# A fused attention and token/channel mixer kernel: load order, the first pairs' engine assignment, and the homes of one addition and three casts

## The chip, the cores and the metric

The kernel runs on one core of a Trainium2 chip. Its time is the device time of one execution in microseconds. Five engines work side by side, each with a queue of its own that runs in order: PE (matrix multiply), DVE (vector), ACT (scalar functions), POOL (GpSimd), and SP, which here only issues DMAs. An engine waits at the head of its queue until what it needs is done; everything behind it waits too.

## The reference

Cosine attention over 8 batches and 12 heads, 448 positions, head size 64, followed by a mixer over tokens and channels:

```python
q_n = q / (norm(q) + 1e-06); k_n = k / (norm(k) + 1e-06)
attn = softmax(q_n @ k_n.T / tau)
x = (attn @ v) rearranged to [batch, 448, 768]
u = x + (relu(x.T @ w_tok1) @ w_tok2).T
out = u + relu(u @ w_ch1) @ w_ch2
```

w_tok1 is 448 x 256 and w_tok2 256 x 448 (the small weights); w_ch1 is 768 x 1536 and w_ch2 1536 x 768. All are float32 in memory; the kernel multiplies in float16.

## The kernel before, in words

**Pairs.** The 96 heads are worked off as 48 pairs (N = 48, six per batch, NPAIR = 6), in a software pipeline whose iteration i does the scores of pair i, the attention output of pair i - 1, and prepares pairs i + 1 to i + 3. The order of all instructions is written out by hand: `tc.manual_schedule()` keeps each engine's queue in program order, and waits are added where data or a buffer is needed.

For one pair the steps are: `load` (q, k, v, 224 KB each, from SP, L164), `squares` (L175 on ACT or L177 on POOL), `norm_sum` (DVE, L187, 16 sums of 64 squares), `norm_root` (ACT, a logarithm and an exponential, L191 and L192), `norm_rec` (DVE, L197 adds 1e-6 and L199 is the reciprocal), `normalize` (q and k times their reciprocal norms into float16, L211), a transpose of both (PE into PSUM, L238, then a copy to `qkT`, by DVE at L246 or ACT at L244), `score` (four matmuls for each half, L257, into two PSUM buffers `pS`), `expo` (ACT, L264, four per pair), `v_cast` (v to float16, by ACT at L220 or by DVE through `recast`, a tensor_reduce over one element, L128), and `pv` (32 matmuls, L278, then DVE's reciprocal at L284 and multiplication into `x` at L285).

**Iterations.** Iterations 0 to 12 are `opening(i)`; from 13 on it is `slot(i)`, where the channel mixer's matmuls of earlier batches (`ch1` L375, `ch2` L384) fill PE between the attention's steps. Batch 0's token mixer is done pair by pair in the opening: `tok1_pair` (L347, L349), `tok2_pair` (L358, into the PSUM tile `pU`) and `u_pair` (L366), which adds `x` to `pU` twice: once into float16 `u16`, which SP then transposes into `uT` (L368), and once into float32 `u32`. In iteration 6 (NPAIR) pairs 4 and 5 are both finished, so four such additions stand in a row. The first `ch1` matmuls follow in iteration 8.

**Before iteration 0** the program lists the loads, and then the norms, the normalization and the transposes of pair 0 and the norms of pair 1. `normalize(0, True)` gives q to POOL in one instruction, and half of k to each of POOL and DVE. The weights go through float32 staging tiles: `w1_load` (eight DMAs, the last 64 rows twice because batches with an odd number use them in the other half of the partitions), `w2_load` (one DMA of 448 KB). They are cast by `w1_cast` (DVE, two instructions at the end of iteration 1) and `w2_cast` (ACT, iterations 1 and 2). w_ch1 and w_ch2 are loaded by POOL's queue (`wide`) in iterations 1 to 11.

The DMAs that SP issues share eight completion counters in turn, so a DMA is issued only after the one eight places earlier has landed. Tiles come from rotating pools: five buffers each for q, k and v, two for `sq`, two for `pS`, four PSUM buffers under the tag `ps` for `pT`, `pO`, `pR`, `pU`, `pG` and `pF`.

Of the kernel before, what the change touches and what calls it, by code (L numbers as in the profile page):

```python
# [9 lines left out]
FP32 = mybir.dt.float32  # L10
FP16 = mybir.dt.float16
AF = mybir.ActivationFunctionType
ALU = mybir.AluOpType
# [5 lines left out]
def _bcast_free(ap: bass.AP, n: int) -> bass.AP:  # L19
    return bass.AP(tensor=ap.tensor, offset=ap.offset, ap=list(ap.ap) + [[0, n]])  # L20
# [3 lines left out]
def kernel(  # L24
# [19 lines left out]
    nc = tc.nc  # L44

    B, H, S, E = q.shape
    D = H * E
    T = moe_w_tok1.shape[1]
    C = moe_w_ch1.shape[1]
    P = 112  # L50
    NCH = S // P
# [3 lines left out]
    NPAIR = H // 2  # L55
# [7 lines left out]
    att = ctx.enter_context(tc.tile_pool(name="att", bufs=3))  # L63
    mix = ctx.enter_context(tc.tile_pool(name="mix", bufs=1))
# [6 lines left out]
        name=nc.get_next_instruction_name(), act_func_set_id=ACT_SET_LN_EXP,  # L71
# [15 lines left out]
    w1t = cst.tile([128, 5, T], FP16, name="w1t")  # L87
# [4 lines left out]
    stage = {}  # L92
# [5 lines left out]
    def ident():  # L98
        nc.gpsimd.memset(id16[:], 0.0)
        nc.gpsimd.affine_select(out=id16[:], in_=id16[:], compare_op=ALU.not_equal,  # L100
                                fill=1.0, base=0, pattern=[[-1, 128]], channel_multiplier=1)
        for t in v16s:
            nc.gpsimd.memset(t[:, :, E:E + 1], 1.0)
        st = mix.tile([128, 5, T], FP32, name="w1s", tag="u32", bufs=2)
        stage["w1"] = st
        nc.gpsimd.memset(st[64:128, 3, :], 0.0)
        nc.gpsimd.memset(st[0:64, 4, :], 0.0)

    def w1_load(n):
        st = stage["w1"]  # L110
        rows = moe_w_tok1.rearrange("(p c) t -> c p t", c=NCH)
        if n < 3:
            for f, m in f_segments(128 * n, 128 * n + 128):
                c, p = f // P, f % P
                nc.sync.dma_start(out=st[f - 128 * n:f - 128 * n + m, n, :],
                                  in_=rows[c, p:p + m, :])
        else:
            nc.sync.dma_start(out=st[0:64, 3, :], in_=rows[3, P - 64:P, :])
            nc.sync.dma_start(out=st[64:128, 4, :], in_=rows[3, P - 64:P, :])

    def w2_load():
        st = mix.tile([128, TT, S], FP32, name="w2s", tag="u32", bufs=2)
# [3 lines left out]
    def recast(out, in_):  # L126

        nc.vector.tensor_reduce(out=out, in_=bass.AP(tensor=in_.tensor, offset=in_.offset,  # L128
                                                     ap=list(in_.ap) + [[1, 1]]),
                                axis=AXX.X, op=ALU.max)  # L130

    def w1_cast(z):
        a, o = (t[:].rearrange("p n t -> p (n t)") for t in (stage["w1"], w1t))
        h = 5 * T // 2
        recast(o[:, z * h:(z + 1) * h], a[:, z * h:(z + 1) * h])

    def w2_cast(tt):
        nc.scalar.copy(out=w2t[:, tt, :].rearrange("k (c p) -> k c p", c=NCH),
# [21 lines left out]
    def load(i, names="qkv"):  # L160
        b, pj = pairs[i]
        for nm in names:
            t = ld.tile([P, 2, NCH, E], FP32, name=f"{nm}l", tag=f"{nm}l")
            nc.sync.dma_start(  # L164
                out=t[:].rearrange("p g c e -> p g (c e)"),
                in_=src[nm][b, 2 * pj:2 * pj + 2].rearrange("g (p c) e -> p g (c e)", c=NCH))
            st_[i][nm] = t

    def squares(i, act=""):
        s = st_[i]  # L170
        s["sq"] = att.tile([P, 2, 2 * NCH, E], FP32, name="sq", tag="sq", bufs=2)
        for j, nm in enumerate("qk"):
            a = s[nm][:].rearrange("p g c e -> p (g c) e")
            if nm in act:
                nc.scalar.activation(out=s["sq"][:, j], in_=a, func=AF.Square)  # L175
            else:
                nc.gpsimd.tensor_mul(out=s["sq"][:, j], in0=a, in1=a)  # L177

    def small(i, nm):
        if nm not in st_[i]:  # L180
            st_[i][nm] = att.tile([P, 2, 2 * NCH], FP32, name=nm, tag=nm)
        return st_[i][nm]

    BOTH = slice(0, 2)

    def norm_sum(i, j=BOTH):
        nc.vector.tensor_reduce(out=small(i, "ssq")[:, j], in_=st_[i]["sq"][:, j], axis=AXX.X,  # L187
                                op=ALU.add)

    def norm_root(i, j=BOTH):  # L190
        nc.scalar.activation(out=small(i, "ln")[:, j], in_=small(i, "ssq")[:, j], func=AF.Ln)  # L191
        nc.scalar.activation(out=nns[i % 3][:, j, :, 0], in_=small(i, "ln")[:, j], func=AF.Exp,  # L192
                             scale=0.5)

    def norm_rec(i, j=BOTH):

        nc.vector.tensor_reduce(out=small(i, "nre")[:, j], in_=nns[i % 3][:, j], axis=AXX.X,  # L197
                                op=ALU.add)
        nc.vector.reciprocal(out=small(i, "rn")[:, j], in_=small(i, "nre")[:, j])  # L199

    def normalize(i, vec):
        s = st_[i]
        t = att.tile([P, 2, NCH, 2, E], FP16, name="qkn", tag="qkn")
        for j, nm in enumerate("qk"):
            for g in ((0, 1) if vec and j else (BOTH,)):
                eng = nc.vector if g == 1 else nc.gpsimd
                rn = small(i, "rn")[:, j].rearrange("p (g c) -> p g c", g=2)[:, g]
                o = t[:, j, :, g, :]
                if g == BOTH:
                    o = o.rearrange("p c g e -> p g c e")  # L210
                eng.tensor_tensor(out=o, in0=s[nm][:, g], in1=_bcast_free(rn, E), op=ALU.mult)  # L211
        s["qkn"] = t

    def v_cast(i, act):
        s = st_[i]
        s["v16"] = v16s[i % 4]
        a = s["v"][:].rearrange("p g c e -> p (g c) e")
        o = s["v16"][:, :, 0:E]
        if act:
            nc.scalar.copy(out=o, in_=a)  # L220
        else:
            recast(o, a)
# [5 lines left out]
            out=s["T"][:].rearrange("d j (c p) -> d (j c) p", c=NCH),  # L228
            in_=s["qkn"][:].rearrange("p j c g e -> p (j c g e)"))

    def tpose_pe(i, act=False):
        s = st_[i]
        s["T"] = att.tile([128, 2, S], FP16, name="qkT", tag="qkT")
        for js in ((slice(0, 1), slice(1, 2)) if act else (BOTH,)):
            pt = ps.tile([128, 2, NCH, P], FP16, name="pT", tag="ps")
            for j in range(js.start, js.stop):
                for c in range(NCH):
                    nc.tensor.transpose(pt[:, j, c, :],  # L238
                                        s["qkn"][:, j, c].rearrange("p g e -> p (g e)"),
                                        id16[:P, :P])  # L240
            o, a = s["T"][:, js].rearrange("d j s -> d (j s)"), \
                pt[:, js].rearrange("d j c p -> d (j c p)")
            if act:
                nc.scalar.copy(out=o, in_=a)  # L244
            else:
                nc.vector.tensor_copy(out=o, in_=a)  # L246

    def score(i, g):

# [177 lines left out]
    todo, held, first = [], [], []  # L427
# [12 lines left out]
    eps()  # L440
    load(1, "qk")
    ident()
    load(0, "v")
    load(2, "qk")
    load(1, "v")
    load(3, "qk")
    for n in range(4):
        w1_load(n)
    w2_load()
    load(4, "qk")  # L450
    for n in (2, 3, 4):
        load(n, "v")
    squares(0, act="qk")
    for j in range(2):
        norm_sum(0, j)
        norm_root(0, j)
    for j in range(2):
        norm_rec(0, j)
    squares(1, act="qk")
    normalize(0, True)  # L460
    tpose_pe(0, act=True)
    norm_sum(1)
    norm_root(1)
    norm_rec(1)
    squares(2)
# [4 lines left out]
    def opening(i):  # L470

        normalize(i + 1, False)
        score(i, 0)
        norm_sum(i + 2)
        expo(i, 0)
        expo(i, 1)
        if not i:
            v_cast(0, True)
        norm_root(i + 2)
        v_cast(i + 1, i in (0, 2, 3, 4, 5))  # L480
        squares(i + 3)
        if i in wide:
            wide[i]()
        fill()
        if i >= 1:
            pv(i - 1, 0)
            pv(i - 1, 1)
        norm_rec(i + 2)
        if i in (1, 2):
            w2_cast(i - 1)  # L490
        r_, u_, add = first[0] if first else (None,) * 3
        done = [i - 2] if 2 <= i <= NPAIR else []
        if done:
            r_(i - 2)
        fill()
        score(i, 1)
        expo(i, 2)
        expo(i, 3)
        tpose_pe(i + 1)
        if i == NPAIR:  # L500
            r_(i - 1)
            done.append(i - 1)
        for pj in done:
            u_(pj)
        for half in (True, False):
            for pj in done:
                add(pj, half)
        if i == 1:
            w1_cast(0)
            w1_cast(1)  # L510
        fill()
        fill()
        fill()
# [98 lines left out]
```

## Time and profile before

| what | us |
|---|---|
| three timed runs | 409.12, 411.62, 411.42; median 411.42 |
| the profiled execution | 409.57 |
| its span in the profile | 407.2 |
| PE busy in the span | 380.6 (93%) |
| DVE, ACT, POOL busy | 233.7, 261.5, 197.9 |

The span runs from the first to the last instruction; 2.4 us of the profiled execution's time lie outside it. A profile line of the timeline gives start, duration, engine, source line, operation, tile written and tile read, shapes, and in brackets how long the engine had stood idle and what ended that. The chain of waits lists, in order of time, the pieces of work and transfers that led to the end: start, length, what. PE is busy for most of the span, but not in the first 76 us: there the busy shares are about 70 to 90% of each slice, and DVE, ACT and POOL are nearly full.

### The profile page before, as it was taken

To read this page: it belongs to the slowest core of one execution; us is meant where nothing else is said; L and a number is where in the kernel's file an instruction comes from. 1 tells how busy PE (TensorE), PEld (TensorE's weight loads), DVE (VectorE), ACT (ScalarE), POOL (GpSimd) and SP (SyncE) were. 2 spreads that over 40 slices of the span, in tenths; PEclk is the share of its full clock that TensorE was granted. 3 is DMA by queue.
4 is the path that set the end of the run, shared out by engine and by line. 5 is a ranking of instruction groups with operands and counts; after the bars stand their busy time and mean duration, and the time that the engine had idled before them with its cause. 6 is when DMAs were issued, how large, how long until landed. Compare 5 with 4: busy or idle time off the path is not lost.

```text
span 407.2 us, 9002 instructions
## 1 busy us (share of the span) xinstructions
PE 380.6 (93%) x3592; PEld 217.7 (53%) x3592; DVE 233.7 (57%) x530; ACT 261.5 (64%) x452; POOL 197.9 (49%) x207
## 2 busy tenths in 40 slices
PE   1778789899999999999999999999999999999996
PEld 1456555555545565555555555555545555655453
DVE  4589988648544775567634766558644773161022
ACT  5979889865677567756686666765677665522400
POOL 4979989825634656543743565634653420000000
PEclk9999999999999999999999999999999999999999
DMA  7899999947963597529864597529962353027023
GB/s 220 239 248 153 267 285 254 254 111 180 222 156 92 149 200 209 153 72 189 239 175 115 138 194 222 137 80 176 249 158 80 73 121 90 2 56 139 0 46 110
DMA packets 97385, 63.63 MB, mean 156 GB/s; under 512 B 57536, under 2 KB 93888, under 8 KB 97344
## 3 DMA queue, kind: packets, MB, share of 16 engines
q1 hardware_dynamic: 94032, 58.20, 59.3%
q0 software_dynamic: 3184, 4.72, 6.8%
q8 instruction: 28, 0.46, 0.5%
q10 hardware_dynamic: 128, 0.15, 0.1%
q14 instruction: 13, 0.11, 0.1%
HBM read 43.45 MB, written 11.01 MB: 134 GB/s over the span
## 4 chain that ended last, share of the span: by engine, by line
PE 80%; DVE 12%; DMA 3%; SPq 2%; ACT 1%; issue 1%; DVEq 0%
PE pG L375 27%; PE pF L384 26%; PE pO L278 9%; PE pS L257 9%; PE pR L309 5%; PE pU L322 3%; DVE ssq L187 2%; DVE x L285 2%; DMA ql<-in_q_dram 2%; DVE qkT L246 2%; DVE u L366 1%; DMA vl<-in_v_dram 1%; SPq L164 1%; DVE u L331 1%; DVE v L128 1%
## 5 line engine op out<-in xcount | busy, mean ns | idle before, releaser
L264 ACT ACTIVATE pE<-pS 112x896 f16<-112x896 f32 x192 | 164.8, 913 | 37.0 <-PE pS L257 36.2
L375 PE MATMUL pG<-uT,wc1t 128*128 128x384 f16 (+1 forms) x576 | 120.5, 353 | 0.0
L384 PE MATMUL pF<-wc2t,gT 128*128 128x384 f16 x672 | 116.6, 326 | 0.2
L211 POOL TENSOR_TENSOR qkn<-ql,rn 112x512 f16<-112x512 f32 x48 | 50.0, 1042 | 134.4 <-DVE rn L199 110.8
L384 PEld LDWEIGHTS <-gT 128*128 128x128 f16 x672 | 63.5, 98 | 47.0 <-issue 7.3
L377 ACT ACTIVATE gT<-pG 128x384 f16<-128x384 f32 (+1 forms) x96 | 52.4, 547 | 44.6 <-PE pG L375 43.7
L375 PEld LDWEIGHTS <-wc1t 128*128 128x128 f16 x576 | 51.3, 97 | 51.1 <-issue 10.4
L388 DVE TENSOR_TENSOR u<-pF,u 128x384 f32<-128x384 f32 x56 | 31.1, 555 | 77.9 <-PE pF L384 77.6
L257 PE MATMUL pS<-qkT 64*112 64x448 f16 x384 | 60.5, 385 | 12.5 <-DVE qkT L246 10.1
L278 PEld LDWEIGHTS <-pE 112*128 112x128 f16 x1536 | 58.2, 99 | 15.7 <-issue 5.1
L278 PE MATMUL pO<-v,pE 112*128 112x65 f16 x1536 | 62.1, 195 | 0.0
L187 DVE TENSOR_REDUCE ssq<-sq 112x16 f32<-112x1024 f32 (+1 forms) x49 | 58.4, 1192 | 5.6 <-ACT sq L175 3.9
L284 DVE RECIPROCAL rec<-pO 128x6 f32<-128x6 f32 x96 | 17.5, 182 | 73.7 <-PE pO L278 72.7
L211 POOL TENSOR_TENSOR qkn<-kl,rn 112x512 f16<-112x512 f32 (+1 forms) x48 | 49.7, 1036 | 0.0
L177 POOL TENSOR_TENSOR sq<-ql 112x512 f32<-112x512 f32 x46 | 48.7, 1058 | 1.1 <-DMA ql<-in_q_dram 1.1
L177 POOL TENSOR_TENSOR sq<-kl 112x512 f32<-112x512 f32 x46 | 48.3, 1051 | 0.0
L285 DVE TENSOR_TENSOR x<-pO,rec 128x384 f16<-128x384 f32 x96 | 40.9, 426 | 3.3
L257 PEld LDWEIGHTS <-qkT 64*112 64x112 f16 x384 | 19.0, 128 | 38.4 <-issue 22.3
L128 DVE TENSOR_REDUCE v<-vl 112x512 f16<-112x512 f32 x39 | 24.9, 639 | 2.6 <-DMA vl<-in_v_dram 2.6
L331 DVE TENSOR_TENSOR u<-pU,x 128x384 f32<-128x384 f32 x50 | 25.4, 546 | 0.1
L337 ACT CAST u<-u 128x768 f16<-128x768 f32 x14 | 11.6, 832 | 20.9 <-DVE u L331 20.9
L191 ACT ACTIVATE ln<-ssq 112x16 f32<-112x16 f32 (+1 forms) x49 | 10.9, 222 | 17.5 <-DVE ssq L187 17.4
(41 smaller groups left out, 182.1 us busy)
## 6 DMA issues: line engine op xcount, KB each, us to landing
ql<-in_q_dram SPq DMA_DIRECT2D x48, 224.0 KB, 3.8
kl<-in_k_dram SPq DMA_DIRECT2D x48, 224.0 KB, 3.8
vl<-in_v_dram SPq DMA_DIRECT2D x48, 224.0 KB, 4.3
out_dram<-u SPq DMA_DIRECT2D x8, 336.0 KB, 3.5
wc1t<-in_moe_w_ch_dram POOLq DMA_DIRECT2D x4, 576.0 KB, 9.7
wc2t<-in_moe_w_ch_dram POOLq DMA_DIRECT2D x3, 768.0 KB, 10.0
out_dram<-u SPq DMA_DIRECT2D x8, 288.0 KB, 4.1
out_dram<-u SPq DMA_DIRECT2D x7, 240.0 KB, 3.0
```

The source lines that it names most:

```text
L177: nc.gpsimd.tensor_mul(out=s["sq"][:, j], in0=a, in1=a)
L187: nc.vector.tensor_reduce(out=small(i, "ssq")[:, j], in_=st_[i]["sq"][:, j], axis=AXX.X, op=ALU.add)
L211: eng.tensor_tensor(out=o, in0=s[nm][:, g], in1=_bcast_free(rn, E), op=ALU.mult)
L257: nc.tensor.matmul(pS[:, h, 0:S], s["T"][64 * h:64 * h + 64, 1, c * P:(c + 1) * P], s["T"][64 * h:64 * h + 64, 0, :], start=True, stop=True)
L264: nc.scalar.activation(out=s["p"][:, c], in_=s["pS"][c][:, :, 0:S], func=AF.Exp, scale=inv_tau)
L278: nc.tensor.matmul(pO[:, n, h, :], s["p"][:, c, h, c0:c0 + 128], s["v16"][:, NCH * h + c, 0:E + 1], start=(c == 0), stop=(c == NCH - 1))
L285: nc.vector.tensor_tensor(out=xt[hp:hp + nr, t0:t0 + len(ts), d0:d0 + 2 * E].rearrange("p t (h e) -> p t h e", h=2), in0=pO[m0:128, :, :, ...
L331: nc.vector.tensor_tensor(out=u32[:, i - t0, cols], in0=pU[:], in1=xt[:, i, cols], op=ALU.add)
L375: nc.tensor.matmul(pG[:], wc1t[:, dt, ct * 128:(ct + 1) * 128], uT[:, dt, :], start=(dt == 0), stop=(dt == DT - 1))
L377: nc.scalar.activation(out=gT[:, ct, :], in_=pG[:], func=AF.Relu)
L384: nc.tensor.matmul(pF[:], gT[:, ct, (i - t0) * 128:(i - t0 + 1) * 128], wc2t[:, ct, dh * DH:(dh + 1) * DH], start=(ct == 0), stop=(ct == C ...
L388: nc.vector.tensor_tensor(out=o, in0=pF[:], in1=o, op=ALU.add)
```

## The change

- **Loads.** The order on SP becomes q, k of pairs 0, 1, 2; v of 0; q, k of 3; v of 1 and 2; q, k of 4; then the small weights w_tok1 and w_tok2; then v of 3 and 4. Before, the small weights stood ahead of q, k of pair 4 and v of 2.
- **w_tok1.** The second copy of the last 64 rows is no longer loaded; the staging tile has four blocks, and POOL's two fills of zeros go to the float16 tile. `w1_cast` has three parts: 128 partitions x 768 elements, 64 x 256, and (in iteration 8) a copy of the last block from the lower to the upper 64 partitions, all on DVE.
- **Pair 0.** `normalize(0)` is done on DVE, q and k one instruction each, and each right after its own reciprocal. POOL has no part in it.
- **ACT.** Pair 1's squares are split: q before the two copies of pair 0's transposes, k between them (`between`). Pair 1's norm sums are two instructions.
- **Casts.** `v_cast` of pairs 0 and 1 moves from ACT to DVE, that of pair 8 from DVE to ACT.
- **The addition.** The float32 addition of pair 5 moves from the end of iteration 6 to the end of iteration 7.

```diff
+    load(2, "qk")
     load(0, "v")
-    load(2, "qk")
+    load(3, "qk")
     load(1, "v")
-    load(3, "qk")
+    load(2, "v")
+    load(4, "qk")
     for n in range(4):
         w1_load(n)
     w2_load()
-    load(4, "qk")
-    for n in (2, 3, 4):
-        load(n, "v")
+    load(3, "v")
+    load(4, "v")
     squares(0, act="qk")
...
-    for j in range(2):
-        norm_rec(0, j)
-    squares(1, act="qk")
-    normalize(0, True)
-    tpose_pe(0, act=True)
-    norm_sum(1)
+    for j, nm in enumerate("qk"):
+        norm_rec(0, j)
+        normalize(0, True, nm)
+    squares(1, act="q", names="q")
+    tpose_pe(0, act=True, between=partial(squares, 1, act="k", names="k"))
+    for j in range(2):
+        norm_sum(1, j)
...
     def w1_cast(z):
-        a, o = (t[:].rearrange("p n t -> p (n t)") for t in (stage["w1"], w1t))
-        h = 5 * T // 2
-        recast(o[:, z * h:(z + 1) * h], a[:, z * h:(z + 1) * h])
+        if z < 2:
+            p, n = (slice(0, 64), slice(3, 4)) if z else (slice(0, 128), slice(0, 3))
+            recast(w1t[p, n, :], stage["w1"][p, n, :])
+        else:
+            recast(w1t[64:128, 4, :], w1t[0:64, 3, :])
...
     def normalize(i, vec, names="qk"):
...
+            eng = nc.vector if vec else nc.gpsimd
+            rn = small(i, "rn")[:, j].rearrange("p (g c) -> p g c", g=2)
+            eng.tensor_tensor(out=t[:, j].rearrange("p c g e -> p g c e"), in0=s[nm][:],
+                              in1=_bcast_free(rn, E), op=ALU.mult)
...
-            v_cast(0, True)
+            v_cast(0, False)
         norm_root(i + 2)
-        v_cast(i + 1, i in (0, 2, 3, 4, 5))
+        v_cast(i + 1, i in (2, 3, 4, 5, 7))
...
+        if i == NPAIR + 1:
+            first[0][2](NPAIR - 1, False)
         for half in (True, False):
             for pj in done:
-                add(pj, half)
+                if half or pj != NPAIR - 1:
+                    add(pj, half)
+        if i == NPAIR + 2:
+            w1_cast(2)
```

## The prediction

> **What bounds the kernel now.** I read the busy shares by slice first, then the chain of waits, then the timeline of the first 76 us.
>
> ```profile
> PE   1778789899999999999999999999999999999996
> DVE  4589988648544775567634766558644773161022
> ACT  5979889865677567756686666765677665522400
> POOL 4979989825634656543743565634653420000000
> ```
>
> A slice is 10.2 us. From about 76 us PE is full to the end, so the change, all of which lies before that, can only make PE's full stretch start earlier or later, and that shift is what the end moves by. In the chain, the first 52 us look like this (start, length, what):
>
> ```profile
> 4.69 6.84 DMA ql<-in_q_dram
> 11.55 0.57 SPq L118
> ...
> 14.44 4.54 DMA vl<-in_v_dram
> ...
> 19.00 0.69 DVE v L128
> ...
> 22.13 0.99 PE pS L257 x3
> 23.12 1.88 PE pO L278 x32
> ...
> 46.27 1.90 DVE u L366 x4
> 48.18 1.12 DVE ssq L187
> 49.30 0.59 DVE v L128
> ```
>
> So v of pair 2, issued at 14.44 behind the small weights, holds DVE until 19.00; and at 46 to 50 DVE's additions, sums and a cast stand in the way of pair 8's scores. The timeline shows the price of both, and one more thing:
>
> ```profile
> 6.37 1.04 POOL L211 TENSOR_TENSOR qkn<-ql,rn 112x512 f16<-112x512 f32 x1 [4.13 <-DVE rn L199]
> 6.87 0.82 DVE L211 TENSOR_TENSOR qkn<-kl,rn 112x256 f16<-112x256 f32 x1
> 7.37 0.79 POOL L211 TENSOR_TENSOR qkn<-kl,rn 112x256 f16<-112x256 f32 x1
> 19.00 0.69 DVE L128 TENSOR_REDUCE v<-vl 112x512 f16<-112x512 f32 x1 [2.63 <-DMA vl<-in_v_dram]
> 52.34 0.59 PE L257 MATMUL pS<-qkT 64*112 64x448 f16 x4 [2.65 <-DVE qkT L246]
> 54.78 0.20 DVE L284 RECIPROCAL rec<-pO 128x6 f32<-128x6 f32 x1 [0.77 <-PE pO L278]
> ```
>
> DVE's 256 elements took 0.82, where 384 take 0.56 elsewhere (L285): it ended 0.28 after POOL's instruction beside it, as if it had begun only then, and POOL's next one (0.79 for half of what takes 1.04) was stretched likewise. [...]
>
> **When things land.** In the trace the 12th to 17th DMA are issued at 7.35, 8.14, 8.97, 9.78, 10.60 and 11.55, which is when the loads eight places earlier land (2.19 + 5.1, 2.69 + 5.4, 3.19 + 5.8, 3.69 + 6.1, 4.19 + 6.4, 4.69 + 6.8). Equal loads land in order, 0.8 apart: place 5 at 8.1, 6 at 9.0, 7 at 9.8, 8 at 10.6, 9 at 11.5, 10 at 12.1. With the new order I keep these times by place: q, k of pair 2 at 8.1 and 9.0 (were 9.0, 9.8), v of 0 at 9.8, v of 1 at 12.1, and on at 0.8 each: v of 2 at 12.9 (was 18.98), q, k of 4 at 13.7 and 14.5. w_tok2 is 21st and can be issued only when the 13th has landed, 14.5; from issue to landing it took 3.7 before, so 18.2. Bounds: 2.7 (the fastest load) and 6.8 (a load in a full queue), so 17.2 to 21.3.
>
> **Pair 0 and ACT's order.** A DVE multiplication of 512 elements from two SBUF inputs isn't in the trace. From 0.56 for 384 and the slope of the sums (1.21 for 1024, 0.69 for 512: 0.13 per 128) it is 0.69; at most 1.64, twice the 256-element row. I take 0.69, since POOL stands idle until q of pair 2 lands. Then q's product runs 6.25 to 6.94 (POOL ended 7.41), k's reciprocal to 7.37, k's product 7.40 to 8.10 (was 8.16). ACT copies q's transpose at 7.6, squares pair 1's k 8.13 to 8.76 (0.63), copies k's to 9.29 (was 9.34): scores start 0.05 earlier. Pair 1's sums end later, 9.5 instead of 9.24, its reciprocal at 10.55 (was 10.24). POOL, however, was busy until 11.08 before and is now free at 10.2, so pair 1's products end at 12.6 instead of 13.1. Squaring pair 2 on POOL must not begin just before k's product: 8.1 against 7.4. If it did, POOL's 1.04 would hold k's product to 8.4, and with the 0.28 of the row above it would end at 8.7, up to 0.65 late.
>
> **Iteration 0.** Two casts of 0.69 join DVE: sums of pair 2 to 12.2 (11.0 + 1.22), casts to 13.6, reciprocal to 14.1, and only then the copy of pair 1's transpose, 14.1 to 14.74. It ended at 14.39: **0.35 lost**. What ACT saves (0.62 + 0.60) finishes pair 0's exponentials at 14.4 instead of 15.0.
>
> **Iteration 1.** From that copy, PE's steps are the path: scores 0.95 (the second half no longer waits for an exponential), 32 pO matmuls 1.9, scores 0.95, transposes 0.93, ending at 19.5. DVE is ready before: its sums and v cast end at 16.7, reciprocals and products take the 1.73 that they took from 19.69 to 21.42, from 17.4 on. So pair 2's copy ends at 20.15 instead of 22.07, **1.9 gained**; the wait of 2.63 is gone and PE's slow matmuls are what comes last. On ACT, w_tok2's cast stands ahead of two exponentials. ACT reaches it at 17.6 and now waits until 18.2; cast 0.98, two exponentials 1.74, to 20.9; the second score buffer is free then, and pair 1's pO starts at 21.45 instead of 23.06: **1.6 of the 1.9 is left**.
>
> **Iteration 2.** w_tok1's casts are 0.94 + 0.42 (0.81 for 640 elements, 1.02 ns each) instead of 1.53; they stand beside PE's pO, as before. PE's steps then keep their lengths. r's activation waits for ACT's v cast and second w2 cast to 25.0 (was 26.45), so I let the shift shrink to **1.5**. Iterations 3 to 5 are untouched, 4.44 each, DVE idle for nothing.
>
> **Iterations 6 to 8.** One addition (0.50) and one cast (0.59) leave DVE's row, so pair 8's copy ends 1.1 earlier. The cast costs ACT 0.60, but its exponentials end at 51.6 instead of 51.4, in time for scores at 51.25 to 51.95. Then comes the first pG group, whose six matmuls wait for six transposes; the last was issued at 48.5 and landed 4.4 later, 52.9, on DVE's additions that stay. It ends at 53.2 instead of 54.0, so 0.8 is left. The moved addition falls into DVE's idle 0.77 before the next reciprocal. In iteration 8 the new copy on DVE (between 0 and 0.42, the 256-element estimate; I take 0.35) leaves 0.7, since DVE waited 0.29 for the transposes after it. From 56.75 POOL runs without a gap, and its start, after pair 10's reciprocal, shifts by the same. **0.7 gained.** Were this cover gone, the addition and the copy would cost 0.85.
>
> **Sum.** 1.5 + 0.7 = 2.2: 409.57 becomes 407.4. The median of the three runs is 1.85 above that execution, and they scatter by 2.5; I put the new median halfway, 0.9 above: **408.3**.
>
> **PE's rate.** The same 32 pO matmuls take 1.94 at 15.61 and 23.06, and 1.15 at 28.82, while the granted clock reads 1.00 in each of these stretches. The trace doesn't say what switches it.
>
> [...] Here 15.61 to 19.34 was busy and stayed slow. [...]
>
> **Rivals.**
> 1. *The fast rate comes earlier.* With 1.15 for pO from iteration 2, and the scores and r at the later 0.59 and 0.61 instead of 0.97 and 1.04, PE's 5.1 there lose 1.6; DVE then allows about 0.8 of it. Gain 3.0, own time 406.6, with the median's offset 407.5. [...]
> 2. *The gain is mostly hidden.* POOL's squares catch k's product (0.65), DVE's two casts delay pair 1 (0.35 already counted), or uT lands later than 52.9 and takes the 0.7. Gain 0.3 to 1.3: 409.2 to 410.2 with the offset.
> 3. *Slower: w_tok2 lands late.* ACT's exponentials stand behind its cast. Beyond 17.7 each microsecond costs one; at 19.85 iteration 1's gain is gone, at 21.3, the upper bound, pO starts 1.45 later than before. Less 0.7: own time 410.3, or 411.2 with the offset, and over 412 if the queue is fuller than any row shows. Against it: 3.7 in a draining queue before.
>
> **How the numbers follow.** Forecast 0.57, rival 1 0.15, rival 2 0.18, rival 3 0.10. The range runs from 405.6 (rival 1 without the offset, and 1.0 less for the scatter) to 411.4 (rival 3 with it); what lies outside is about 2 in 10. One per cent is 4.1 us, about what a measurement of this kernel can tell from no change. Faster by more, below 407.3, is most of rival 1 and the forecast if the runs fall like the profiled one: 0.21. Slower by more, above 415.5, needs rival 3 beyond its bound: 0.04. Within 1%: 0.75.
>
> **What would show it.** DVE's v cast of pair 2 without a wait, near 16; its copy for pair 2 ending near 20.2, for pair 1 near 14.7; ACT's w2 cast waiting for a DMA until about 18.2; iteration 8's first score near 49.8 (51.25 less 1.5) and PE full from about 73.5. The prediction is wrong if ACT waits past 19.8 for w_tok2, if k's product of pair 0 takes more than 0.8, or if the first pG group still starts where pair 8's copy was late before.

## The result, and the profile after

| what | before | after |
|---|---|---|
| median of 22 runs each, us | 410.45 | 408.51 |
| ratio, 95% interval | | 0.9935 [0.9914, 0.9956] |
| the profiled execution | 409.57 | 408.18 |
| its span | 407.2 | 406.0 |
| end of DVE's copy for pair 3, 7, 8, 9, 13 | 27.91, 46.27, 52.28, 57.25, 75.62 | 25.97, 44.44, 49.39, 55.95, 74.45 |

The ratio is a gain of 2.7 us, with 1.8 to 3.5 in the interval; 408.3 was forecast. The medians are over all 22 runs, the ratio leaves out two slow ones of the kernel after (412.18 and 412.85; with them the means differ by 2.3). Some of the gain isn't in the span at all: what a run's time has beyond its span is 2.4 to 2.5 us in the kernel before and 2.15 in the kernel after, so 0.3 of it comes from outside, which no edit was meant to touch and no run explains.

The last row is the ruler for all that follows: it says when DVE has copied a pair's transposes to `qkT`, the last step before that pair's scores. Behind pair 13's copy lie 331.5 us in the kernel before and 331.5 to 332.0 in all others but two (332.4 and 333.5), so a microsecond there is a microsecond at the end of the span.

The busy shares after, by slice of 10.15 us, with the granted clock of PE:

```profile
PE   2798799899999999999999999999999999999996
DVE  5879978557544765467634766558644773161022
ACT  6799879865767557856687567756676665521400
POOL 3979979826544647443734655644653520000000
PEclk9999989999999999999999999999999999999999
```

DVE's second slice is 8 where it was 5: the wait for v of pair 2 is gone. The 8 in PEclk, in the sixth slice, was not there before. The chain of waits after, pieces of its first 46 us (start, length, what):

```profile
2.69 4.94 DMA ql<-in_q_dram
7.64 5.87 DMA kl<-in_k_dram
13.53 3.95 DMA w2s<-in_moe_w_tok_dram
17.51 0.99 ACT w2t L139
18.50 1.64 ACT pE L268 x2
20.13 0.04 issue
20.18 0.62 PE pS L261 x2
20.80 1.88 PE pO L282 x32
...
44.44 1.44 DVE u L370 x3
45.88 1.13 DVE ssq L190
```

Where v of pair 2 stood, w_tok2 stands now: its cast holds ACT, ACT's exponentials hold PE. In the late stretch DVE has three additions instead of four ahead of pair 8's sums, and the cast behind them is gone. The timeline after (start, duration, engine, line, operation, in brackets the idle time before it and what ended it):

```profile
5.77 0.69 DVE L213 TENSOR_TENSOR qkn<-ql,rn 112x512 f16<-112x512 f32 x1
6.81 0.69 DVE L213 TENSOR_TENSOR qkn<-kl,rn 112x512 f16<-112x512 f32 x1
15.18 0.68 DVE L127 TENSOR_REDUCE v<-vl 112x512 f16<-112x512 f32 x1
17.51 0.99 ACT L139 CAST w2t<-w2s 128x448 f16<-128x448 f32 x1 [1.01 <-DMA w2s<-in_moe_w_tok_dram]
20.73 1.94 PE L282 MATMUL pO<-v,pE 112*128 112x65 f16 x32
49.45 0.63 PE L261 MATMUL pS<-qkT 64*112 64x448 f16 x4 [1.59 <-DVE qkT L248]
50.02 2.10 PE L379 MATMUL pG<-uT,wc1t 128*128 128x384 f16 x6
```

Pair 0's products take 0.69 each, v of pair 2 is cast without a wait, ACT waits 1.01 for w_tok2, and iteration 8's scores start at 49.45, after PE stood idle for 1.59 (before: at 52.34, after 2.65). But the first pG group takes 2.10, and before it took 1.15:

```profile
52.86 1.15 PE L375 MATMUL pG<-uT,wc1t 128*128 128x384 f16 x6
```

The windows view after shows why (columns: stretch, its length, busy time of PE, PEld, DVE, ACT and POOL with the number of instructions, granted PE clock, DMA share, GB/s):

```profile
48.00:49.00 1.00, 0.00 (x0) 0.00 (x0) 0.90 (x4) 1.00 (x3) 0.81 (x2) 1.00 1.95 254
49.00:50.00 1.00, 0.55 (x4) 0.30 (x4) 1.00 (x3) 0.74 (x2) 1.00 (x2) 0.99 0.82 207
50.00:51.00 1.00, 1.00 (x6) 0.49 (x5) 1.00 (x2) 1.00 (x2) 1.00 (x2) 0.50 1.14 207
51.00:52.00 1.00, 1.00 (x6) 0.50 (x5) 0.58 (x1) 0.94 (x3) 1.00 (x2) 0.50 1.10 219
52.00:53.00 1.00, 1.00 (x21) 1.00 (x20) 0.00 (x0) 0.49 (x1) 0.93 (x1) 0.50 1.11 217
```

At 50.0, just behind an idle stretch of PE (47.86 to 49.45), the granted clock falls to half for 3.4 us. Pair 9's copy comes 6.56 behind pair 8's, 4.97 before: 1.59 of what had been gained is lost. In this execution 1.83 was gained at pair 7, 2.89 at pair 8, 1.30 at pair 9 and 1.17 at pair 13, and 1.2 is what the span lost.

### The profile page after: what moved, and what is told of

Its sections match the earlier page's. It is cut to its first block, busy times and chain, and to the rows that moved or that the text cites. A ratio compares the mean times of both kernels' runs of the same rounds, so it can differ in the third digit from the quotient of the medians.

```text
span 406.0 us, 8998 instructions
## 1 busy us (share of the span) xinstructions
PE 382.7 (94%) x3592; PEld 219.4 (54%) x3592; DVE 234.7 (58%) x534; ACT 261.5 (64%) x451; POOL 196.2 (48%) x205
## 4 chain that ended last, share of the span: by engine, by line
PE 81%; DVE 12%; DMA 4%; ACT 2%; issue 1%; SPq 0%; DVEq 0%
PE pG L379 27%; PE pF L388 27%; PE pO L282 10%; PE pS L261 9%; PE pR L313 5%; PE pU L326 3%; DVE ssq L190 2%; DVE x L289 2%; DMA kl<-in_k_dram 1%; DVE qkT L248 1%; DVE u L370 1%; ACT pE L268 1%; DMA ql<-in_q_dram 1%; DMA w2s<-in_moe_w_tok_dram 1%; DVE u L335 1%; DVE rec L288 1%
## 5 line engine op out<-in xcount | busy, mean ns | idle before, releaser
L213 POOL TENSOR_TENSOR qkn<-ql,rn 112x512 f16<-112x512 f32 x47 | 49.0, 1043 | 130.6 <-DVE rn L202 109.6
L379 PEld LDWEIGHTS <-wc1t 128*128 128x128 f16 x576 | 51.6, 98 | 51.4 <-issue 11.0
L288 DVE RECIPROCAL rec<-pO 128x6 f32<-128x6 f32 x96 | 17.5, 182 | 76.1 <-PE pO L282 75.2
L180 POOL TENSOR_TENSOR sq<-ql 112x512 f32<-112x512 f32 x46 | 48.7, 1058 | 5.6 <-DMA ql<-in_q_dram 5.6
L213 POOL TENSOR_TENSOR qkn<-kl,rn 112x512 f16<-112x512 f32 x47 | 49.0, 1042 | 0.0
L180 POOL TENSOR_TENSOR sq<-kl 112x512 f32<-112x512 f32 x46 | 48.3, 1051 | 0.0
L194 ACT ACTIVATE ln<-ssq 112x16 f32<-112x16 f32 (+1 forms) x49 | 10.9, 222 | 17.5 <-DVE ssq L190 17.2
```

The costliest lines, as they stand in the source:

```text
L213: eng.tensor_tensor(out=t[:, j].rearrange("p c g e -> p g c e"), in0=s[nm][:], in1=_bcast_free(rn, E), op=ALU.mult)
L379: nc.tensor.matmul(pG[:], wc1t[:, dt, ct * 128:(ct + 1) * 128], uT[:, dt, :], start=(dt == 0), stop=(dt == DT - 1))
```

## The experiments

No kernel leaves work out; those with extra matmuls write them into a PSUM tile that has been read already, or, at the start of `e6_pe_kept_busy`, into one of their own. Ratios are to the kernel before, times of copies are from the one profiled execution of each kernel. A ratio also holds the time outside the span: 2.4 to 2.5 us in the kernel before, e1, e2, e7, e9 and e12, 2.15 in after, e3 and e4, 1.8 in e5, e6, e8, e10 and e11. So up to 0.7 us of a ratio's gain (0.0017) is no gain of the pipeline, and the copies are the better measure.

**Loads alone** (`e1_loads_alone`): the kernel before with the new order, w_tok1 still in eight DMAs.

```diff
-    load(0, "v")
     load(2, "qk")
+    load(0, "v")
+    load(3, "qk")
     load(1, "v")
-    load(3, "qk")
+    load(2, "v")
+    load(4, "qk")
     for n in range(4):
         w1_load(n)
     w2_load()
-    load(4, "qk")
-    for n in (2, 3, 4):
-        load(n, "v")
+    load(3, "v")
+    load(4, "v")
```

> The kernel before with the new load order alone (w_tok1 still in eight DMAs and five blocks). Theory A, the parts add up and the load order carries the gain of iterations 1 and 2: DVE's v cast of pair 2 runs without its wait of 2.63, pair 2's copy to qkT ends near 19.5 (22.07 before, 19.07 with the whole change), ACT waits for w_tok2 until 17.5 to 18.5, and pair 8's copy ends 1.5 to 2.0 earlier than the 52.28 of before; gain 1.5 to 2.0 us. Theory B, the front's other edits (pair 0 on DVE, ACT's order, the casts of pairs 0 and 1 on DVE) are needed for it, because ACT with two casts more and a wait for w_tok2 becomes the late one: pair 2's copy not before 20.5, gain under 1 us.

Ratio 0.9973 [0.9950, 0.9997]. In its timeline v of pair 2 no longer makes DVE wait, but

```profile
15.35 0.59 SPq L124 DMA_DIRECT2D w2s<-in_moe_w_tok_dram  x1
15.46 0.68 DVE L128 TENSOR_REDUCE v<-vl 112x512 f16<-112x512 f32 x1
19.68 1.00 ACT L138 CAST w2t<-w2s 128x448 f16<-128x448 f32 x1 [2.97 <-DMA w2s<-in_moe_w_tok_dram]
```

w_tok2 is issued 1.8 later than in the kernel after (13.53) and ACT waits 2.97 for it. Pair 2's copy comes at 19.71 (22.07 before), pair 3's at 27.78, only 0.13 earlier: the wait has moved from DVE to ACT. So the first theory is right of DVE's wait and of pair 2, the second of what is left behind it. (The ratio leaves 0.1 to 2.1 us of gain where this execution shows 0.1 at pair 8.) Rival 3 was right of this half of the change, if not to the point of a loss. The rest of the change must make w_tok2 land sooner.

**Late moves alone** (`e2_late_alone`): the addition and pair 8's cast.

```diff
-        v_cast(i + 1, i in (0, 2, 3, 4, 5))
+        v_cast(i + 1, i in (0, 2, 3, 4, 5, 7))
...
+        if i == NPAIR + 1:
+            first[0][2](NPAIR - 1, False)
         for half in (True, False):
             for pj in done:
-                add(pj, half)
+                if half or pj != NPAIR - 1:
+                    add(pj, half)
```

> The kernel before with only the late moves: pair 5's float32 addition an iteration later, pair 8's v cast on ACT. Theory A: nothing changes up to pair 7; pair 8's copy ends 1.1 earlier (51.2 instead of 52.28), of which 0.7 to 1.1 reach the end, unless PE falls to half rate after its idle stretch there; gain 0.7 to 1.1 us. Theory B, the gain is hidden because the first pG group waits for the last transpose of uT, landed at 52.9: the group ends near 54.0 as before, gain under 0.3 us.

Ratio 0.9967 [0.9942, 0.9992]. From pair 7's copy to pair 8's 4.95 instead of 6.01: 1.06 gained. So it is in all nine kernels with these moves (4.94 to 4.97), and the five without them have 6.01 or 6.02. The granted clock fell to 0.50 twice in this execution, at 21.0 to 27.8 and at 51.7 to 55.1, so its span of 407.6 shows nothing of the gain.

**The whole change with the old load order** (`e3_front_and_late`).

```diff
-    load(2, "qk")
     load(0, "v")
-    load(3, "qk")
+    load(2, "qk")
     load(1, "v")
-    load(2, "v")
-    load(4, "qk")
+    load(3, "qk")
     for n in range(4):
         w1_load(n)
     w2_load()
-    load(3, "v")
-    load(4, "v")
+    load(4, "qk")
+    for n in (2, 3, 4):
+        load(n, "v")
```

> The whole change with the old load order put back. Theory A, the load order carries the early gain: v of pair 2 makes DVE wait until about 19 again, pair 2's copy ends at 21.7 to 22.1, and only the late moves' gain of 0.7 to 1.1 us is left (about 409.5 where before has 410.45). Theory B, the front's edits carry it: pair 2's copy ends before 20.5 and the gain stays above 1.7 us.

Ratio 0.9953 [0.9930, 0.9977]. Pair 2's copy at 20.60, between the two expectations, and pair 3's at 26.75: 1.16 gained without the new load order. DVE waited 1.7 for v of pair 2, not 2.63. Two things could do that, pair 0's new homes or the missing eighth DMA of w_tok1; the next four runs part them.

**Loads, and w_tok1 in seven DMAs** (`e7_loads_w1_seven`), and **seven DMAs alone** (`e9_w1_seven_alone`, with the old order).

```diff
-            nc.sync.dma_start(out=st[64:128, 4, :], in_=rows[3, P - 64:P, :])
...
     def w1_cast(z):
-        a, o = (t[:].rearrange("p n t -> p (n t)") for t in (stage["w1"], w1t))
-        h = 5 * T // 2
-        recast(o[:, z * h:(z + 1) * h], a[:, z * h:(z + 1) * h])
+        if z < 2:
+            p, n = (slice(0, 64), slice(3, 4)) if z else (slice(0, 128), slice(0, 3))
+            recast(w1t[p, n, :], stage["w1"][p, n, :])
+        else:
+            recast(w1t[64:128, 4, :], w1t[0:64, 3, :])
...
+        if i == NPAIR + 2:
+            w1_cast(2)
```

> The new load order alone, plus w_tok1 in seven DMAs with its three casts as in the whole change; the front and the late moves are those of before. With eight DMAs ACT waited 2.97 for w_tok2, to 19.65. Theory A, the eighth DMA took a turn of the eight counters, so that w_tok2 had to wait for the first of w_tok1's own to land: with seven it is issued 1.0 to 1.8 earlier (near 14.0), ACT's wait falls to 1.0 to 1.8, and pair 3's copy ends at 26.3 to 27.0 instead of 27.78. Theory B, w_tok2 lands late because the queue is full, not because of its turn: it still lands after 19, pair 3's copy within 0.3 of 27.78.

> The kernel before with one edit: w_tok1 in seven DMAs (the last 64 rows loaded once, a third cast copies them in iteration 8), the load order as before. Theory A: the eighth DMA itself is what made later loads wait. Without it v of pair 2 is issued about 1.4 earlier (13.0 instead of 14.44), pair 2's copy ends at 20.4 to 20.9 (22.07 before), pair 3's at 26.5 to 27.1 (27.91), less 0.3 for the third cast: 0.6 to 1.2 us less, a ratio of 0.997 to 0.9985. Theory B: the 1.15 us that the kernel with the old load order had gained at pair 7 came from pair 0 and ACT's order: pair 3's copy at 27.7 or later here, ratio 0.999 to 1.001.

Ratios 0.9974 [0.9951, 0.9996] and 0.9975 [0.9954, 0.9996]. With both edits w_tok2 is issued at 13.37 instead of 15.35 and the timeline has

```profile
16.90 1.00 ACT L139 CAST w2t<-w2s 128x448 f16<-128x448 f32 x1 [0.16 <-DMA w2s<-in_moe_w_tok_dram]
```

a landing 2.8 earlier for one DMA of 64 KB less. (Some 0.8 of that isn't its doing: in the run of the loads alone, SP's queue was that much later already at k of pair 4, 8.11 against 7.35.) Pair 3's copy is at 25.60, 2.31 gained, against 0.13 with the order alone. With seven DMAs alone, v of pair 2 is issued 0.96 earlier (13.48 for 14.44) and lands 1.1 earlier:

```profile
17.31 0.99 ACT L139 CAST w2t<-w2s 128x448 f16<-128x448 f32 x1
17.88 0.69 DVE L127 TENSOR_REDUCE v<-vl 112x512 f16<-112x512 f32 x1 [1.30 <-DMA vl<-in_v_dram]
```

Pair 3's copy at 26.12, earlier than its own expectation; part of that is PE's rate, below. Where the time of the first kernel leaves 0.2 to 2.0 us of gain, its profile has 2.16 at pair 13 (73.46): one execution, not the median.

**Pair 0, ACT's order and the casts of pairs 0 and 1 alone** (`e10_front_alone`): the kernel before with these edits.

```diff
-    for j in range(2):
-        norm_rec(0, j)
-    squares(1, act="qk")
-    normalize(0, True)
-    tpose_pe(0, act=True)
-    norm_sum(1)
+    for j, nm in enumerate("qk"):
+        norm_rec(0, j)
+        normalize(0, True, nm)
+    squares(1, act="q", names="q")
+    tpose_pe(0, act=True, between=partial(squares, 1, act="k", names="k"))
+    for j in range(2):
+        norm_sum(1, j)
...
-            v_cast(0, True)
+            v_cast(0, False)
-        v_cast(i + 1, i in (0, 2, 3, 4, 5))
+        v_cast(i + 1, i in (2, 3, 4, 5))
```

> The kernel before with pair 0's products on DVE, ACT's copies and squares in turn, and the casts of v of pairs 0 and 1 on DVE; loads, w_tok1 and the late moves as before. Theory A: these edits take nothing off the path, since pair 1's copy ends later on DVE for the two casts (14.4 to 14.8) and pair 2's waits for v of 2 as before: pair 3's copy at 27.6 to 28.2 (27.91 before), ratio 0.999 to 1.001. Theory B: they bring the 1.15 at pair 7: pair 3's copy at 26.9 or earlier, ratio 0.996 to 0.998.

Ratio 0.9987 [0.9965, 1.0009], pair 3's copy at 28.01 (27.91 before): nothing on the path. The mean span of its runs is 408.7, that of the kernel before beside it 408.8; the ratio's 0.5 us lies outside the span. So the 1.16 of the kernel with the old load order came from the eighth DMA, as `e9_w1_seven_alone` shows by itself.

**w_tok2 later** (`e8_w2_later`): the whole change, w_tok2 behind v of 3 and 4.

```diff
     for n in range(4):
         w1_load(n)
-    w2_load()
     load(3, "v")
     load(4, "v")
+    w2_load()
```

> The whole change with w_tok2's DMA behind v of pairs 3 and 4. Theory A, the third rival's price holds, one microsecond for each that w_tok2 is late: it lands 1.0 to 2.0 later than 17.48, ACT's wait grows from 1.01 to 2.0 to 3.0, and pair 3's copy ends later by the same, 27.0 to 28.0, so that the gain of iterations 1 and 2 is gone; ratio to before 0.996 to 0.999. Theory B, the landing hardly moves because the loads share the bandwidth, or PE's slow matmuls hide it: pair 3's copy before 26.5, ratio near that of the change, 0.9935.

Ratio 0.9987 [0.9963, 1.0012]. The cast starts 2.53 later than after,

```profile
20.04 0.99 ACT L139 CAST w2t<-w2s 128x448 f16<-128x448 f32 x1 [2.81 <-DMA w2s<-in_moe_w_tok_dram]
```

and pair 3's copy 2.44 later (28.41 for 25.97): 0.96 us for each. At 20.04 the early gain is gone and 0.5 more; in the runs the mean span is 408.1, as in those of the kernel before beside it. That is rival 3 in place and price; a line through the two kernels puts the turning point at 19.5, where 19.85 was reckoned.

**w_tok2 ahead of w_tok1** (`e5_w2_ahead`).

```diff
+    w2_load()
     for n in range(4):
         w1_load(n)
-    w2_load()
     load(3, "v")
```

> The whole change with w_tok2's one DMA ahead of w_tok1's seven. Theory A, ACT's wait for w_tok2 (1.01 in the changed kernel, to 17.48) is the last late thing of iteration 1: w_tok2 is then issued near 8.5 and lands by 16.5, ACT casts at 16.5 without a wait, iteration 2's scores no longer wait for ACT's exponentials, pair 3's copy ends 0.6 to 1.0 earlier (25.97 in the changed kernel), and so does the end: ratio to before about 0.992. Theory B, the wait was hidden behind PE's slow matmuls or w_tok1, now later, holds DVE's casts at 19 instead: pair 3's copy within 0.3 of 25.97.

Ratio 0.9920 [0.9889, 0.9951]. ACT casts w_tok2 at 16.71 without a wait and pair 3's copy ends at 24.06, 1.91 earlier than after. Not all of that is w_tok2's doing: PE was at the full rate from 18.9 here (32 pO matmuls in 1.15 at 19.95), in the kernel after only from 26.1 (1.94 at 20.73; last section). `e7_loads_w1_seven`, where w_tok2 was cast at 16.90 and the full rate came at 24.4, had 25.60, so PE's rate is the likelier cause of most of it. Then the clock fell from 25.7 to 29.1 and pair 4's copy ended at 30.61, where after had 30.52: all given back. It fell again at 49.6.

**The gap of iteration 7 filled** (`e4_fill_gap`): the whole change, and eight matmuls of 390 columns while PE waits for pair 8's copy.

```diff
+    def keep_busy(pO):
+        o = pO[:].rearrange("p t h e -> p (t h e)")
+        for _ in range(8):
+            nc.tensor.matmul(o, w2t[:, 0, 0:128], w2t[:, 0, 0:6 * (E + 1)], start=True, stop=True)
...
         if i == NPAIR + 1:
+            keep_busy(st_[i - 1]["pO"])
             first[0][2](NPAIR - 1, False)
```

> The whole change, and eight extra matmuls of 390 columns in iteration 7, between the transposes of pair 9's predecessor (pair 8) and its scores, where PE stands idle from 47.9 to 49.45; their result is not used. In the profile of the changed kernel the granted clock fell to 0.50 at 50.0, for 3.5 us, and the first pG group took 2.04 instead of 1.08. Theory A, the clock falls because a stretch of about 3.4 us before it held too little PE work (1.6 us): with the gap filled it stays at 1.00 through 50 to 54, the pG group takes 1.1, the time falls by 1.0 to 1.7 us against the changed kernel (406.8 to 407.5), and scatters less. Theory B, the fall has to do with something other than PE's idleness: the clock still falls in that stretch, or the time is that of the changed kernel, 408.5, or above it by the matmuls' length if they overrun the gap.

Ratio 0.9923 [0.9892, 0.9954]. The windows view of this kernel, same columns as above:

```profile
48.00:49.00 1.00, 0.78 (x6) 0.29 (x5) 0.97 (x3) 0.98 (x2) 0.82 (x2) 1.00 1.63 155
49.00:50.00 1.00, 1.00 (x8) 0.53 (x6) 1.00 (x2) 0.77 (x1) 1.00 (x2) 1.00 1.10 136
50.00:51.00 1.00, 0.98 (x20) 0.67 (x18) 0.92 (x2) 1.00 (x3) 1.00 (x2) 1.00 1.17 187
```

No fall here. Pair 9's copy comes 5.20 behind pair 8's instead of 6.56, so useless work on PE gains 1.36 in this execution against that of the kernel after. Pair 13's ends at 72.44 and the span is 404.1; the other 0.65 against after lies ahead of the fill. That the fill is what kept the clock up is borne out by the other profiles: none of the four kernels with the gap filled has a fall after 30.1, and eight of the ten others have one that begins between 49 and 54. The runs don't resolve the gain: the ratios of the two kernels differ by less than their intervals.

**PE kept busy from the start as well** (`e6_pe_kept_busy`): w_tok2 ahead, the filled gap, and some 70 small matmuls before and between the first scores.

```diff
+    warm(45)
     squares(0, act="qk")
...
+            if act:
+                warm(5 if js.start else 3)
             if between and not js.start:
                 between()
```

> As the kernel with w_tok2 ahead, with the eight extra matmuls in iteration 7, and more extra matmuls whose result isn't used: 45 of 128 columns ahead of pair 0's transposes, 3 and 5 behind them, 5 and 9 in iteration 0, 2 of 390 columns in iteration 1, all where PE stood idle. Theory A, PE's rate follows its own occupancy over stretches of 3.4 us, from the first microsecond on: pO of pairs 0 and 1 takes about 1.15 instead of 1.94, scores 0.59 instead of 0.99, pair 3's copy ends 1.0 to 2.0 earlier than with w_tok2 ahead alone, no stretch at 0.50 in iterations 7 to 9, and the time is the lowest of all, 405.0 to 406.5 where before has 410.45. Theory B, the start is slow whatever PE does, or the extra matmuls, at the slow rate, overrun the gaps: pO stays at 1.94 and pair 2's copy ends later than 19.07.

Ratio 0.9922 [0.9892, 0.9952]. Pair 0's pO took 1.39 and pair 1's 1.15 instead of 1.94 each. But the added matmuls stood in PE's queue ahead of pair 0's scores (9.92, where they start at 8.7 to 9.5 in the other kernels), the clock fell at 9.6 to 16.4 and 26.7 to 30.1, and pair 3's copy ended at 24.20, no earlier than `e5_w2_ahead`'s 24.06 without them. This is also one of the two kernels whose stretch behind pair 13 differs (333.5): PE waited 1.8 there for a DMA transpose. (In `e12_no_front_fill`, 332.4, it waited 0.7 for one.)

**Two versions put together**: `e11_w2_ahead_fill` is the kernel after with w_tok2 ahead and the gap filled; `e12_no_front_fill` is the kernel before with the new loads, seven DMAs, the late moves and the filled gap, so the whole change without the edits of `e10_front_alone`.

```diff
# e11_w2_ahead_fill, from the kernel after
+    w2_load()
     for n in range(4):
         w1_load(n)
-    w2_load()
...
         if i == NPAIR + 1:
+            keep_busy(st_[i - 1]["pO"])
             first[0][2](NPAIR - 1, False)
```

> The kernel after with w_tok2 ahead of w_tok1, and eight matmuls of 390 columns in iteration 7's gap on PE. If the two add up: no fall of the clock near 50, pair 7's copy at 44.0 to 44.6 or, where no fall comes between 25 and 30 either, near 42.5; pair 13's at 72.0 to 73.2, 3 to 3.8 us less than before and a ratio of 0.990 to 0.992. If a fall of the clock between 21 and 30 takes what w_tok2 ahead brings, as in the runs of each: no better than either alone, 0.992 to 0.9935.

> The kernel before with the new load order, w_tok1 in seven DMAs, the addition and pair 8's cast moved, and the eight matmuls in iteration 7's gap: the whole change without its edits of pair 0, of ACT's order and of the casts of pairs 0 and 1. Theory A: those edits bring nothing, so this is the kernel after with the gap filled: pair 7's copy at 43.8 to 44.5, pair 13's at 72.2 to 73.2, ratio 0.9905 to 0.993. Theory B: they are worth half a microsecond or more: ratio 0.994 or above, pair 7's copy past 44.9.

Ratios 0.9885 [0.9849, 0.9920] and 0.9923 [0.9902, 0.9944]. The first has the lowest median of all, 406.57 us (411.34 for the kernel before beside it); its profiled execution (406.46) had a fall at 24.9 to 28.3, which took most of what had been gained by then (pair 3's copy 23.80, pair 4's 30.19), and none at 50; pair 13's copy is at 72.66. It is ahead of the kernel before; that it is ahead of the kernel after too is likely and not shown, since its interval overlaps that of after's own ratio and `e4_fill_gap`'s, and 0.4 us of its lead over either lies outside the span. The second has pair 7's copy at 43.73 and pair 13's at 72.20, no later than `e4_fill_gap` with 43.78 and 72.44: it needs neither pair 0's new homes nor ACT's order.

## Why the prediction was right, and where it wasn't

The time was right; its terms less so, and two errors cancelled.

- **Pair 0 and ACT's order.** 0.69 for 512 elements on DVE was right to the hundredth. POOL's first square for pair 2 (L180) started at 7.80, behind k's product (6.81 to 7.50), so rival 2's 0.65 wasn't lost. No run shows that term: it was the author's estimate from the one row of before where 256 elements on DVE took 0.82 beside POOL's 1.04, and in the kernel after the two did not overlap. Scores 0.05 earlier and pair 1's copy 0.35 later were too small to see: pair 1's copy ends at 13.83 to 14.60 in the six kernels with pair 0 as before, and at 13.70 to 14.43 in those with its new homes alone. In the kernel after k of pair 0 landed early enough that its square ran at 4.07 instead of 4.56, so its 13.70 (14.74 predicted) owes half a microsecond to the loads of that one execution.
- **When things land.** The step failed in size. Kept by place, the 13th DMA was to land at 14.5 and w_tok2 at 18.2; w_tok2 was issued at 13.53 and landed at 17.48. So ACT waited until 17.5 and pair 1's pO started at 20.73, not 21.45.
- **The eighth DMA of w_tok1** stood in that count of places but was given no price of its own. It is what the early gain hangs on: the same order gains 0.13 at pair 3 with it, 2.31 without. In the place that the order gives them, w_tok2 is the 22nd DMA with it and waits for the first of the small ones, which itself was issued at 8.9; as the 21st it waits for k of pair 4, issued at 7.26 to 7.76 in the four kernels that have it so.
- **Iterations 1 and 2.** Predicted shift 1.5. At pair 7 it was 1.83 after, 2.49 with the gap filled (the fill comes later, so that is the same early program), 2.31 to 2.54 in the two kernels without pair 0's edits. So the term was 0.3 to 1.0 too small: w_tok2 landed 0.7 sooner than reckoned, and where PE turned fast early, its rate added to that.
- **Iterations 3 to 5** kept 4.44 each (30.52 to 34.96 to 39.40).
- **Iterations 6 to 8.** Pair 8's copy: 1.06, predicted 1.1. Where the clock doesn't fall (`e4_fill_gap`), pair 9's copy gives 0.23 back (the first pG group took 1.33 instead of 1.15, by the forecast's reasoning for the last part of `uT`), pair 10's 0.30 to the new copy (0.41 on DVE, predicted 0.35), pair 11's returns 0.16: 0.69, predicted 0.7.
- **PE's rate**, left open, is the term that spoilt the sum of the profiled execution. Own time 407.4 was predicted, 408.18 measured. Its copies show 1.83 gained by pair 7 and would show 1.83 + 0.69 = 2.5 at pair 13, 0.3 more than the 2.2 predicted; the fall took 1.36 of it. `e4_fill_gap`, with no fall there, gained 2.49 + 0.69 = 3.2 and took 406.26.
- **From own time to median.** An offset of 0.9 was added; 0.33 was right. That and the 0.8 of the rate made up for each other. The offset has a cause now: the profiled execution of before had no fall of the clock, most others had. Its runs have a mean granted clock of 0.991 to 0.993 against 0.998 for the profiled one; after's have 0.992, and the three kernels with the gap filled and nothing added to the start 0.997 to 0.998. In the 82 runs of the kernel before that have a clock beside them, the 16 at 0.998 or more have a mean span of 407.2, the other 66 one of 409.1. What was not in the sum at all is the 0.3 that the time outside the span fell by.
- **Rivals.** 1 does happen: PE was fast from 17.5 to 18.9 on in six of the kernels (e2, e4, e5, e9, e11, e12), but in each a fall of the clock followed 3.4 or 6.8 later. The stretch from 15.61 to 19.34, which the prediction notes as busy and still slow (3.72 of 3.73 busy), lay across two windows of the kernel before (12.94 to 16.36 and 16.36 to 19.77, by the steps of the last section), with 2.46 and 2.98 of 3.41 busy: neither was full, and in these runs windows up to 2.98 left the rate slow. 2 didn't. 3 has its price confirmed, and the seven DMAs kept it away.

The first score of iteration 8 was forecast near 49.8 and came at 49.45; pair 13's copy was to be ready near 73.4 (75.62 less 2.2) and was at 74.45, the fall being what lies between.

## What to carry to other kernels

A load order is worth what its last load allows: before moving weights to the back, find who waits for them, and count the DMAs in the queue one by one, since a small one costs a place like a large one (the new order gained 0.13 at pair 3 with the eighth DMA of w_tok1, of 64 KB, and 2.31 without it). When an idle gap on PE is shortened, look at the granted clock behind it: what is gained can go to the half rate, and cheap matmuls in the gap can bring it back (1.36 in one profile here, not resolved by the runs). Compare two profiles only after the falls of the clock in each have been marked; medians of runs carry the average of them.

## What the hardware showed that was not expected

The granted clock falls to 0.50 for 3.4 us, or for 6.8. (A fall behind PE's last work, at 404.97 in after and at 405.48 in before, is not counted here.) The kernels by the numbers in their names, with the time at which the first stretch at the full rate begins, the falls, and PE's busy time in the 3.41 us ahead of each fall:

| kernel | full rate from, us | falls, us | PE busy in the 3.41 before |
|---|---|---|---|
| after | 26.1 | 50.0 to 53.4 | 1.60 |
| e1 | 26.5 | 53.8 to 57.2 | 1.57 |
| e2 | 17.5 | 21.0 to 27.8, 51.7 to 55.1 | 0.75, 1.60 |
| e3 | 25.9 | 49.8 to 53.2 | 1.95 |
| e4 | 18.1 | 21.6 to 25.0 | 2.01 |
| e5 | 18.9 | 25.7 to 29.1, 49.6 to 53.0 | 1.34, 1.60 |
| e6 | 6.2 | 9.6 to 16.4, 26.7 to 30.1 | 1.34, 1.90 |
| e8 | 27.5 | 51.4 to 54.8 | 1.97 |
| e9 | 18.9 | 22.4 to 25.8, 49.7 to 56.5 | 1.73, 1.72 |
| e10 | 27.3 | 51.2 to 58.0 | 1.78 |
| e11 | 18.1 | 24.9 to 28.3 | 1.72 |
| e12 | 18.1 | 21.5 to 24.9 | 2.02 |
| before | 26.6 | none | |
| e7 | 24.4 | none | |

Where one execution has two falls, their starts lie 30.7, 23.9, 17.1 and 27.3 us apart: 9.0, 7.0, 5.0 and 8.0 times 3.413, the length in us of the one fall in after (49.98 to 53.40). All 16 falls begin a whole number of such steps, 1 to 10, after the time in the second column. Laid out in such steps, in these 14 executions windows at full rate with 2.28 us or more busy were never followed by a fall. At the slow rate (the falls, and the start of each execution), windows with up to 2.98 left it there and windows with 3.29 or more ended it; between 3.04 and 3.23 both happened. In after PE stood idle for 1.59 in one piece and was busy for 1.60 of the window, and the clock fell; ahead of the second fall of e6 1.90 were busy and the longest idle piece was 0.8. So in these runs a window that is half busy was mostly not enough to keep the clock up (three exceptions stand below).

The slow rate at the start is the rate of the falls, and follows the same steps: the 32 pO matmuls take 1.94 in both, at 15.05 in e2, ahead of its first record, and at 22.46, where the record reads 0.50. The views read 1.00 at the start, but only because the trace holds no record of the clock before the first stretch at the full rate, and a time without a record counts as full: the times in the second column are where the records begin. In the kernel before that is 26.60, and the 32 pO matmuls of the prediction took 1.94 at 15.61 and 23.06, ahead of it, and 1.15 at 28.82, behind it. So the trace does show when the rate switched. `e9_w1_seven_alone` had a full window ending at 18.9, then one with 1.73, behind which the granted clock fell, then one with 3.39. Its timeline has the rate of the 32 pO matmuls before, across and after:

```profile
15.82 1.94 PE L279 MATMUL pO<-v,pE 112*128 112x65 f16 x32
21.52 1.30 PE L279 MATMUL pO<-v,pE 112*128 112x65 f16 x32
27.43 1.15 PE L279 MATMUL pO<-v,pE 112*128 112x65 f16 x32
```

In after the windows end at 19.3, 22.7 and 26.1 with 2.56, 3.12 and 3.34, and PE stays slow until 26.1. So the fast rate came at 18.9 where the window that ended there was full (3.41), and at 26.1 where the one that ended at 19.3 had 2.56.

What stays open is which of PE's work counts. Three windows at the full rate had no more busy time than those ahead of the falls, and no fall followed: before, ending at 53.9, with 1.56, e7, ending at 51.7, with 1.68, and e6, ending at 84.7, with 1.62, though windows with up to 2.02 fell elsewhere. To leave the transposes `pT` out of the busy time does not part them: 15 of the 16 falls then have 1.57 or less, and these three windows keep 1.56, 1.68 and 1.62; but the second fall of e6 then still has 1.90, and before's 1.56 is below that of one window that a fall followed (e1, 1.57). No run was made to settle it.
